# Eight of sixteen first-layer groups in seven products of halves, in place of four, with the steps of a block put in a new order

## The chip, the core and the metric

The kernel runs on one core of a Trainium2 chip. The metric is the device time of one execution, in microseconds (us). The engines are named as the profile names them: PE multiplies matrices, PEld loads its weights, DVE, ACT and POOL are the vector, scalar and general engines, SP only issues DMAs here. Each engine works through its own instructions in order and waits on semaphores for the others.

## The reference

Linear attention with projected keys and values over eight batches, and behind it a feed-forward layer on all tokens. With B = 8 batches, H = 8 heads, S = 1024 tokens, D = 64 and k = 64 projected positions:

```python
k_proj = einsum('ks,bhsd->bhkd', E, k)
v_proj = einsum('ks,bhsd->bhkd', F, v)
attn = softmax(q @ k_proj^T / sqrt(D))          # over the 64 projected positions
x = (attn @ v_proj) as 8192 tokens of H*D = 512
h = x @ w_in                                    # 512 -> 2048
g = h * clip(h + 3, 0, 6) / 6
out = g @ w_out                                 # 2048 -> 512
```

The kernel computes in bf16 with float32 sums; inputs are cast while they are loaded, the output is float32.

## The kernel before

**Blocks.** Each batch b has two blocks, t = 0 and t = 1, of 512 tokens; "block (b,t)" below. PE is kept fed by an order written out by hand: a string of step names such as `L0 A7 L1 A6`, walked once per block. A letter names a piece of work, the number says which part of it. `at(place, ...)` hangs further work (the attention of the next batch) behind a named step, `pop()` after a step takes one postponed instruction from the list `later`, and `behind_steps(n)` postpones an instruction by n steps (the list `soon`, counted down by `step_done`).

**First layer.** A block's h has 2048 columns, done as 16 groups of 128: `first_group` (L0 to L15) is 8 matmuls of 512 columns into a PSUM tile of the pool `ps_mm` (tag "mm", four tiles). `h_out` then makes g from it: ACT writes r = relu(h/6 + 0.5) to a tile of the pool `rpool`, DVE multiplies g = min(r, 1) * h.

**Second layer.** g times w_out for the tokens of a block is done on 2x2 blocks of halves with seven products in place of eight (Strassen's scheme in Winograd's form). `Pair` does this for two of the four rows of output tiles: steps 7, 2, 5, 6, 1, 3 and 4 are the seven products. It needs sums of blocks of g (class `Sums`: a in place on DVE, sb on DVE, sc and sd on POOL) and of w_out (`w_sums`, and b12 and b21 in place). Steps 7, 2 and 5 are copied from PSUM to SBUF by ACT (`copied`, m7, m2, m5), and steps 6, 1, 3 and 4 make the output tiles o_sb of the pool `opool` by a subtraction on DVE or a copy on ACT; each tile is stored by an SP DMA. The second layer of a block runs while the next block's first layer is computed: A and B are the two pairs of the block before, N is the pair A of the present block, of which steps 2 and 5 are done early (N2, N5).

**Quad.** From batch 3 on, four of the sixteen groups (f = 12 to 15) are done together by the same scheme, in seven products of halves: `Quad`, steps Q7, Q2, Q6, Q5, Q1, Q3, Q4, each 8 matmuls of 256 columns. Its sums of x (xc, xa, xb, xd) are made on POOL by `sums`, its sums of w_in lie in `v_sums`, and two blocks of w_in (v12, v21) are replaced by their sums in place in batch 3. Steps 7, 2 and 5 are copied to float32 tiles qm7, qm2, qm5 by ACT; steps 6, 1 and 3 subtract on DVE, and then g is made from the result: Relu on ACT, min and multiply on POOL. Step 4 goes Relu on ACT, multiply on DVE.

**Attention of the next batch.** `second` is the attention whose x is made during this batch: `some_scores` (PE) and exponents (ACT, line 276, from PSUM tiles of the pool `ps_at`, tag "at"), `add_up` (a transposing reduction on DVE, line 308), `sums_turned` (small DVE instructions), `spread_sums` (a reciprocal on DVE, two SP DMAs that write turned_rows to DRAM, eight SP DMAs that spread it over partitions as rec), and in t = 1 `some_values` (PE, then multiplies by rec on DVE, line 300, which give xT). `third` is the attention after that: `projected` is 32 pairs of matmuls on k and v; behind it, one step at a time, the casts of kp (ACT), `turn` (three SP transposing DMAs: kT, and qT twice) and the casts of vp. `load_next` issues the DMAs of the next k, v and q from POOL, behind a small copy, the mark, that waits for qT.

The order of the blocks of batches 3 to 7, and what hangs on it:

```python
    QUADS = ("L0 A7 L1 A6 L2 B7 L3 A1 L4 B2 L5 A3 L6 B5 L7 A4 "
             "L8 Q7 Q2 B6 L9 Q6 N2 Q5 B1 L10 Q1 B3 L11 Q3 N5 B4 Q4").split()
...
            at((0, "L1"), scores(0, 1))
...
            spread((0, "B6"), (0, "B3"))
            if third:
                at((0, "B4"), lambda: third.projected(pause=False))
                if third.b + 1 < B:
                    at((1, "L7"), third.load_next)
```

After the last block the remaining steps of the second layer run in the order `TAIL`. Batches 1 and 2 have the order `ORDER` (the first block `START`), without quads.

Of the kernel before, what the change touches and what calls it, by code (L numbers as in the profile page):

```python
# [15 lines left out]
def kernel(  # L16
# [41 lines left out]
    gpool = ctx.enter_context(tc.tile_pool(name="g", bufs=2))  # L58
    rpool = ctx.enter_context(tc.tile_pool(name="r", bufs=4))
    spool = ctx.enter_context(tc.tile_pool(name="s", bufs=1))  # L60
    opool = ctx.enter_context(tc.tile_pool(name="o", bufs=4))
    ps_mm = ctx.enter_context(tc.tile_pool(name="ps_mm", bufs=4, space=bass.MemoryType.PSUM))
# [75 lines left out]

    NQ, KX = 2, KO // 2
    v11, v12, v21, v22 = [w_in_sb[:, k:k + KX, f * P:(f + NQ) * P] for k in (0, KX) for f in (FO - 2 * NQ, FO - NQ)]  # L140
    v_sums = consts.tile([P, 3, KX, NQ * P], bf16, name="v_sums")

    def sums_of_w_in():
        add(v_sums[:, 0], v11, v21, nc.gpsimd)
        add(v_sums[:, 1], v11, v22, nc.gpsimd)
        sub(v_sums[:, 2], v11, v12, nc.gpsimd)

# [74 lines left out]
    class Attention:  # L222
# [91 lines left out]
        def sums_turned(self):  # L314
            turned, other = [att.tile([P, KO * 32], f32, tag="turned", name="turned", bufs=2) for _ in range(2)]
            inv = att.tile([KP, KO * 32], f32, tag="inv", name="inv", bufs=1)
            nc.vector.transpose(turned, self.parts.rearrange("p j c -> p (j c)"))
            for t in range(NB):
                here, there = slice(t * KP, t * KP + 32), slice(t * KP + 32, (t + 1) * KP)
                nc.vector.tensor_copy(other[here], turned[there])  # L320
                nc.vector.tensor_add(inv[t * 32:(t + 1) * 32], turned[here], other[here])
            self.inv = inv
# [410 lines left out]
    class Quad:  # L733

        def __init__(self, x, t, g, last):
            self.g, self.last = g, last
            self.blocks = [x[:, k:k + KX, t, i * HT:(i + 1) * HT] for i in range(2) for k in (0, KX)]

        def sums(self):
            a11, a12, a21, a22 = self.blocks
            tiles = [spool.tile([P, KX, HT], bf16, tag="x" + name, name="x" + name) for name in "cabd"]
            self.xc, self.xa, self.xb, self.xd = tiles
            add(self.xc, a11, a21, nc.gpsimd)
            sub(self.xa, a22, a21, nc.gpsimd)
            sub(self.xb, a11, self.xa, nc.gpsimd)
            sub(self.xd, a12, self.xb, nc.gpsimd)

        def product(self, n, ps, first=False):  # L750
            a11, a12, a21, a22 = self.blocks
            x, w = {1: (self.xb, v_sums[:, 1]), 2: (a11, v_sums[:, 2]), 3: (self.xd, v22), 4: (a12, v21),
                    5: (self.xc, v12), 6: (self.xa, v11), 7: (a22, v_sums[:, 0])}[n]
            for p in range(NQ):
                for k in range(KX):
                    in_columns(ps[:, p * HT:(p + 1) * HT], w[:, k, p * P:(p + 1) * P], x[:, k],
                               start=(first and p == k == 0), stop=(k == KX - 1),
                               skip_group_check=not first or p > 0)

        def copied(self, name):  # L760
            m = spool.tile([P, TOK], f32, tag="q" + name, name="q" + name)
            nc.scalar.copy(m, self.y)
            return m

        def out(self, h, i, j, engine=None):
            f = FO - 2 * NQ + j * NQ
            g = self.g[:, f:f + NQ, i * HT:(i + 1) * HT]

            def relu():
                r = rpool.tile([P, TOK], f32, tag="r", name="r")  # L770
                nc.scalar.activation(r, h, AF.Relu, bias=0.5, scale=1.0 / 6.0)  # L771
                r3, h3 = [v.rearrange("p (a n) -> p a n", a=NQ) for v in (r, h)]
                if self.last or engine is nc.vector:
                    behind_steps(1)(lambda: nc.vector.scalar_tensor_tensor(g, r3, 1.0, h3, op0=ALU.min, op1=ALU.mult))
                else:
# [5 lines left out]
        def step(self, n):  # L781
            if n in (7, 2):
                self.y = pat()
            elif n == 6:
                self.x = pmm()
            self.product(n, self.y if n in (7, 2, 5) else self.x, n in (7, 2, 6))
            if n == 7:
                self.m7 = self.copied("m7")
            elif n == 2:
                self.m2 = self.copied("m2")  # L790
            elif n == 5:
                self.m5 = self.copied("m5")
            elif n == 6:
                sub(self.m7, self.m7, self.x)
                self.out(self.m7, 1, 0, nc.gpsimd)
            elif n == 1:
                sub(self.m5, self.m5, self.x)
                self.out(self.m5, 1, 1, nc.gpsimd)
            elif n == 3:
                sub(self.m2, self.x, self.m2)  # L800
                self.out(self.m2, 0, 1, nc.gpsimd)
            else:
                self.out(self.x, 0, 0, nc.vector)
# [15 lines left out]
    for what in "A2 A7 V0 B7 A5 V1 A6 R B2 A1 V2 B5 R A3 B6 V3 A4 B1 R".split():  # L819
# [11 lines left out]
        if what in added:  # L831
# [3 lines left out]


    ORDER = ("L0 A7 L1 A6 L2 B7 L3 A1 L4 B2 L5 A3 L6 B5 L7 A4 "
             "L8 L9 B6 L10 N2 L11 B1 L12 N5 L13 B3 L14 L15 B4").split()
    QUADS = ("L0 A7 L1 A6 L2 B7 L3 A1 L4 B2 L5 A3 L6 B5 L7 A4 "
             "L8 Q7 Q2 B6 L9 Q6 N2 Q5 B1 L10 Q1 B3 L11 Q3 N5 B4 Q4").split()  # L840
    START = "L0 B3 L1 L2 B4 L3 L4 L5 L6 L7 L8 L9 L10 N2 L11 L12 L13 N5 L14 L15".split()
    TAIL = "A7 B7 B2 A6 B5 B6 A1 B1 A3 B3 A4 B4".split()

    second = Attention(2)
    for b in range(1, B):
        if b + 1 < B:
            x_next = second.xT = x_tile()
# [31 lines left out]
        elif b == 2:  # L879
# [7 lines left out]
            at((1, "A6"), add_up(3))  # L887
            spread((1, "A1"), (1, "L4"))
            at((1, "L4"), third.projected)
        elif b + 1 < B:  # L890
            if b == 3:
                at((0, "L0"), lambda: add(v12, v12, v22, nc.gpsimd), lambda: sub(v21, v21, v22, nc.gpsimd))
                at((0, "start"), second.load_next)
            at((0, "L1"), scores(0, 1))
            at((0, "B7"), add_up(0))
            at((0, "A1"), scores(2, 3), add_up(1))
            at((0, "A3"), add_up(2))
            at((0, "A4"), add_up(3))
            spread((0, "B6"), (0, "B3"))
            if third:  # L900
                at((0, "B4"), lambda: third.projected(pause=False))
                if third.b + 1 < B:
                    at((1, "L7"), third.load_next)
        if b < 3:
# [6 lines left out]
        elif b + 1 < B:  # L911
            at((1, "L3"), values(0, 1))
            at((1, "L7"), values(2, 3))

# [3 lines left out]

        for t in range(NB):
            g = g_tile()  # L920
            sums = Sums(g)
# [3 lines left out]
            if quads:  # L925
                pairs["Q"] = Quad(xT, t, g, (b, t) == (B - 1, NB - 1))
            if not start:
                behind[0].sums.a(KH - left, KH)
            left = 2 * NQ if quads else 2
            done("start")  # L930
            for what in START if start else QUADS if quads else ORDER:
                n = int(what[1:])
                if what[0] != "L":
                    pairs[what[0]].step(n)
                    step_done()
                    if quads and what[0] in "LQB":
                        pop()
                    done(what)
                    if what == ("N5" if quads else "N5" if start else "B3"):
                        sums.a(0, KH - left)  # L940
                    continue
# [7 lines left out]
                else:  # L949
                    first_group(xT, t, g, n, behind_steps(2) if quads and n >= KH else now)  # L950
                step_done()
                pop()
                if n == KH - 1:
                    sums.c()
                if not start and n == 0:
                    behind[0].sums.b()
                    behind[0].sums.d()
                if quads and n == 0:
                    pairs["Q"].sums()
                done(what)  # L960
            while soon:
                step_done()
# [4 lines left out]
    sums = behind[0].sums  # L967
    sums.a(KH - left, KH)
    sums.b()
    sums.d(nc.vector)  # L970
    for what in TAIL:
        behind["AB".index(what[0])].step(int(what[1:]))

# [29 lines left out]
```

## Time and profile before

| | |
|---|---|
| median of 3 runs | 480.58 us (480.12 to 480.73) |
| the profiled execution | 480.11 us, of which the span is 478.3 us |
| PE busy | 471.1 us, 99%, 6450 matmuls |
| DVE busy | 340.0 us, 71%, 549 instructions |
| POOL busy | 304.4 us, 64%, 206 instructions |
| ACT busy | 275.1 us, 58%, 532 instructions |
| a first-layer group's Relu (ACT, L562), mean | 598 ns |
| its multiply (DVE, L563), mean | 680 ns |
| a quad's min on POOL (L776), mean | 1536 ns |
| a quad's multiply on POOL (L777), mean | 1345 ns |

The profile is one execution. Times in it are counted from the start of the span; the execution's own time is 1.8 us longer than the span. Busy time of the vector engines is the sum of the instructions' durations; where two instructions follow each other without a wait, the record of the second begins a little ahead of the end of the first. The blocks of batches 3 to 7 begin at 191.35, 219.76 (batch 3), 246.81, 275.66 (4), 302.70, 331.55 (5), 358.58, 385.70 (6), 412.73 and 438.37 us (7); the tail begins at 464.45 us. In a listing, L199 is line 199 of the kernel; `mm<-xT,w_in_sb` reads "writes mm, reads xT and w_in_sb".

### The profile page before, as it was taken

The numbers are of one execution on the slowest core, as the hardware profiler recorded it, in microseconds if no ns is written. First come the engines' busy times: TensorE is split into PE (matmuls) and PEld (weight loads), VectorE is DVE, ScalarE is ACT, GpSimd is POOL, SyncE is SP. The second block draws the span as 40 slices with busy tenths as digits, with TensorE's granted clock in tenths as the row PEclk, the third lists the DMA queues.
The fourth block names the chain that finished last, engine by engine and source line by source line (L and its number), as shares of the span: only waits on it lengthen the run. The fifth ranks groups of instructions, "written<-read, shape, count | busy, mean of one in ns | idle before, by whom it ended". The sixth has DMA issues, their size and how long they took to land.

```text
span 478.3 us, 14964 instructions
## 1 busy us (share of the span) xinstructions
PE 471.1 (99%) x6450; PEld 347.1 (73%) x6450; DVE 340.0 (71%) x549; ACT 275.1 (58%) x532; POOL 304.4 (64%) x206
## 2 busy tenths in 40 slices
PE   8899999999999999999999999999999999999997
PEld 4454567667666776787787877778687877878797
DVE  3583387678765958886778867887778897747574
ACT  3666478775447554756466555666457554556451
POOL 8634956144335123877897778887778588788820
PEclk9999999999999999999999999999999999999999
DMA  9999989984976989995999197962931054111012
GB/s 165 197 201 207 239 148 209 161 152 95 226 148 109 208 158 223 201 202 135 222 143 194 48 210 144 209 135 67 210 117 45 24 151 120 45 47 45 30 62 89
DMA packets 84593, 68.65 MB, mean 144 GB/s; under 512 B 38320, under 2 KB 70576, under 8 KB 84528
## 3 DMA queue, kind: packets, MB, share of 16 engines
q0 software_dynamic: 33008, 29.36, 39.4%
q1 hardware_dynamic: 51152, 37.83, 33.0%
q8 instruction: 50, 0.82, 0.7%
q10 hardware_dynamic: 368, 0.52, 0.4%
q14 instruction: 15, 0.12, 0.1%
HBM read 71.83 MB, written 16.97 MB: 186 GB/s over the span
## 4 chain that ended last, share of the span: by engine, by line
PE 82%; DMA 7%; DVE 4%; POOL 2%; ACT 2%; issue 2%; SPq 1%; POOLq 0%; ACTq 0%
PE mm L199 60%; PE at L199 19%; DMA v<-in_v_dram 5%; DMA rec<-turned_rows 1%; PE at L288 1%; DVE g L563 1%; PE at L267 1%; DVE parts L308 1%; ACT aT L276 1%; SPq L335 1%; POOL q L103 1%; POOL k L107 1%; DMA turned_rows<-inv 0%; POOL v L107 0%; DVE xT L300 0%
## 5 line engine op out<-in xcount | busy, mean ns | idle before, releaser
L199 PE MATMUL mm<-xT,w_in_sb 128*64 128x512 bf16 (+1 forms) x1808 | 222.3, 375 | 0.0
L563 DVE SCALAR_TENSOR_TENSOR g<-r,mm 128x512 bf16<-128x512 f32 x216 | 146.1, 680 | 70.8 <-ACT r L562 69.8
L562 ACT ACTIVATE r<-mm 128x512 f32<-128x512 f32 x216 | 128.3, 598 | 114.6 <-PE mm L199 109.0
L199 PEld LDWEIGHTS <-w_in_sb 128*64 128x64 bf16 x2048 | 118.9, 110 | 58.3 <-issue 3.2
L199 PEld LDWEIGHTS <-g 128*64 128x64 bf16 x2048 | 113.5, 110 | 23.9 <-issue 4.1
L133 POOL TENSOR_TENSOR sc<-g 128x2048 bf16<-128x2048 bf16 x14 | 57.0, 4072 | 53.0 <-DVE g L563 53.0
L136 POOL TENSOR_TENSOR sd<-g,sb 128x1024 bf16<-128x1024 bf16 x28 | 59.0, 2126 | 42.4 <-DVE sb L136 40.0
L199 PE MATMUL mm<-w_out_sb,g 128*64 128x256 bf16 (+1 forms) x1088 | 78.1, 286 | 0.1
L199 PE MATMUL at<-w_sums,g 128*64 128x256 bf16 x896 | 59.0, 273 | 0.2 <-DVE g L563 0.2
L776 POOL TENSOR_SCALAR r<-r 128x512 f32<-128x512 f32 x27 | 41.5, 1536 | 15.2 <-ACT r L771 15.2
L692 ACT COPY m<-at 128x256 f32<-128x256 f32 x84 | 31.3, 373 | 32.8 <-PE at L199 28.1
L777 POOL TENSOR_TENSOR g<-r,qm 128x512 bf16<-128x512 f32 x27 | 36.3, 1345 | 2.3
L300 DVE TENSOR_TENSOR xT<-at,rec 128x512 bf16<-128x512 f32 x54 | 34.9, 682 | 2.6 <-DMA rec<-turned_rows 1.9
L199 PE MATMUL mm<-w_out_sb,sd 128*64 128x256 bf16 x480 | 31.4, 273 | 0.1
L136 DVE TENSOR_TENSOR o_sb<-m,mm 128x256 f32<-128x256 f32 x60 | 24.7, 412 | 9.5 <-PE mm L199 7.2
L199 PE MATMUL mm<-w_sums,sb 128*64 128x256 bf16 x480 | 31.3, 273 | 0.0
L276 ACT ACTIVATE aT<-at 128x512 bf16<-128x512 f32 x52 | 29.5, 602 | 2.9 <-PE at L267 2.9
L199 PEld LDWEIGHTS <-sd 128*64 128x64 bf16 x480 | 26.9, 110 | 4.0 <-issue 0.4
L308 DVE TRANSPOSE_TENSOR_REDUCE parts<-aT 128x32 f32<-128x1024 bf16 x24 | 29.6, 1234 | 0.0
L199 PE MATMUL at<-w_out_sb,sc 128*64 128x256 bf16 x448 | 29.6, 273 | 0.0
L199 PEld LDWEIGHTS <-sc 128*64 128x64 bf16 x480 | 26.7, 110 | 3.6 <-issue 0.5
L199 PEld LDWEIGHTS <-sb 128*64 128x64 bf16 x480 | 26.2, 110 | 4.2 <-issue 1.9
(115 smaller groups left out, 496.1 us busy)
## 6 DMA issues: line engine op xcount, KB each, us to landing
out_dram<-o_sb SPq DMA_DIRECT2D x60, 256.0 KB, 4.4
rec<-turned_rows SPq DMA_DIRECT2D x48, 256.0 KB, 5.8
k<-in_k_dram POOLq DMA_DIRECT2D x7, 1024.0 KB, 10.6
v<-in_v_dram POOLq DMA_DIRECT2D x7, 1024.0 KB, 16.3
q<-in_q_dram POOLq DMA_DIRECT2D x7, 1024.0 KB, 21.1
w_out_sb<-in_moe_w_out_dram POOLq DMA_DIRECT2D x4, 512.0 KB, 15.0
w_in_sb<-in_moe_w_in_dram POOLq DMA_DIRECT2D x7, 256.0 KB, 9.7
k<-in_k_dram POOLq DMA_DIRECT2D x4, 256.0 KB, 5.6
```

The lines of the kernel that those rows point to most:

```text
L103: nc.gpsimd.dma_start(out=q0[:, t, hs], in_=kqv_dram["q"][0][:, hs, t * SB:(t + 1) * SB, :])
L133: engine.tensor_tensor(out=out, in0=x, in1=y, op=ALU.add)
L136: engine.tensor_tensor(out=out, in0=x, in1=y, op=ALU.subtract)
L199: nc.tensor.matmul(ps[lo:lo + width], stationary[:, lo:lo + width], moving, **flags)
L276: when(lambda r=r: nc.scalar.activation(aT[:, :, r, :], tiles[r].rearrange("p (a n) -> p a n", a=2), AF.Exp, scale=scale))
L300: when(lambda t=t: nc.vector.tensor_mul(self.xT[:, j, t, :], av[t], rec[:, t]))
L308: nc.vector.tensor_reduce(out=self.parts[:, j], op=ALU.add, axis=mybir.AxisListType.X, apply_transpose=True, in_=self.aT[j].rearrange("p a ...
L562: nc.scalar.activation(r, h_ps, AF.Relu, bias=0.5, scale=1.0 / 6.0)
L563: when(lambda: nc.vector.scalar_tensor_tensor(g[:, fo, :], r, 1.0, h_ps, op0=ALU.min, op1=ALU.mult))
L692: self.copy(m, ps)
L776: nc.gpsimd.tensor_scalar(out=r, in0=r, scalar1=1.0, scalar2=None, op0=ALU.min)
L777: nc.gpsimd.tensor_tensor(out=g, in0=r3, in1=h3, op=ALU.mult)
```

## The change

From batch 3 on a second quad, R, takes groups f = 8 to 11, so that a block has L0 to L7 and two times seven products of halves. Both quads of a block use the same sums of x. The sums of w_in are made for both (in batch 1), the in-place ones for R in batch 2. The last two steps of Q (q3, q4) are done in the next block or the tail. The second factor of g's clip is now done differently: Q's three subtracted blocks have Relu on ACT, and min and multiply in one instruction on DVE; R's steps 6 and 1 have a second Relu on ACT (1 - relu(0.5 - h/6), clipped at 0) and a multiply on POOL, its step 3 is as Q's. The sum a of g is one DVE instruction of 128x2048, in the next block, in place of two of 128x1024. The sums of a block are made at new places (`MADE`), the x tile of the next batch is taken later, and several pools are smaller: r and o_sb three tiles in place of four, `turned` one in place of two, qm2 two in place of one.

The order of the steps, and the places at which the attention's parts hang, are new for these blocks. The core of the diff (left out: the passing of engines to `Quad`, the change of `sums_turned` that writes over `parts`, and places where only names change):

```diff
-    rpool = ctx.enter_context(tc.tile_pool(name="r", bufs=4))
+    rpool = ctx.enter_context(tc.tile_pool(name="r", bufs=3))
...
-    opool = ctx.enter_context(tc.tile_pool(name="o", bufs=4))
+    opool = ctx.enter_context(tc.tile_pool(name="o", bufs=3))
...
-    NQ, KX = 2, KO // 2
+    NQ, KX, NQUADS = 2, KO // 2, 2
+    v_blocks = [[w_in_sb[:, k:k + KX, f * P:(f + NQ) * P] for k in (0, KX) for f in (FO - (2 * i + 2) * NQ, FO - (2 * i + 1) * NQ)]
+                for i in range(NQUADS)]
...
+    def sums_in_place(i):
+        v11, v12, v21, v22 = v_blocks[i]
+        add(v12, v12, v22, nc.gpsimd)
+        sub(v21, v21, v22, nc.gpsimd)
...
-        def copied(self, name):
-            m = spool.tile([P, TOK], f32, tag="q" + name, name="q" + name)
+        def copied(self, name, y):
+            m = spool.tile([P, TOK], f32, tag="q" + name, name="q" + name, bufs=2 if name == "m2" else 1)
...
-                nc.scalar.activation(r, h, AF.Relu, bias=0.5, scale=1.0 / 6.0)
+                nc.scalar.activation(r, h, AF.Relu, bias=0.5, scale=(-1.0 if engine is nc.scalar and not self.last else 1.0) / 6.0)
...
-                if self.last or engine is nc.vector:
-                    behind_steps(1)(lambda: nc.vector.scalar_tensor_tensor(g, r3, 1.0, h3, op0=ALU.min, op1=ALU.mult))
+                if engine is nc.scalar and not self.last:
+                    nc.scalar.activation(r, r, AF.Relu, bias=1.0, scale=-1.0)
+                    nc.gpsimd.tensor_tensor(out=g, in0=r3, in1=h3, op=ALU.mult)
+                elif self.last or engine is nc.vector:
+                    behind_steps(2)(lambda: nc.vector.scalar_tensor_tensor(g, r3, 1.0, h3, op0=ALU.min, op1=ALU.mult))
...
-    QUADS = ("L0 A7 L1 A6 L2 B7 L3 A1 L4 B2 L5 A3 L6 B5 L7 A4 "
-             "L8 Q7 Q2 B6 L9 Q6 N2 Q5 B1 L10 Q1 B3 L11 Q3 N5 B4 Q4").split()
+    QUADS = ("L0 q3 L7 A7 L5 q4 L1 B7 A6 L3 L2 L6 A1 B2 R7 L4 B6 B5 "
+             "A3 R2 R6 B1 R5 N2 A4 Q2 R1 Q7 Q6 B3 Q5 R3 Q1 N5 R4 B4").split()
+    MADE = {'L1': 'x', 'R2': 'c', 'q3': 'a', 'B2': 'd', 'A6': 'b'}
+    LAST = {'q3': 'ab', 'A6': 'd'}
+    ENGINES = ((nc.vector, nc.vector, nc.vector), (nc.scalar, nc.scalar, nc.vector),)
...
-    TAIL = "A7 B7 B2 A6 B5 B6 A1 B1 A3 B3 A4 B4".split()
+    TAIL = ("q3 B2 q4 A7 B7 A6 B6 "
+             "A1 B5 B1 A3 B3 A4 B4").split()
...
-        if b + 1 < B:
+        if b + 1 < B and b < 4:
             x_next = second.xT = x_tile()
...
-            at((0, "L1"), scores(0, 1))
-            at((0, "B7"), add_up(0))
-            at((0, "A1"), scores(2, 3), add_up(1))
-            at((0, "A3"), add_up(2))
+            at((0, "q3"), scores(0, 1))
+            at((0, "L6"), add_up(0))
+            at((0, "L3"), scores(2, 3))
+            at((0, "B5"), add_up(1))
+            at((0, "R7"), add_up(2))
             at((0, "A4"), add_up(3))
-            spread((0, "B6"), (0, "B3"))
+            spread((0, "Q2"), (0, "Q6"))
             if third:
-                at((0, "B4"), lambda: third.projected(pause=False))
+                at((0, "Q2"), lambda: third.projected(pause=False))
                 if third.b + 1 < B:
-                    at((1, "L7"), third.load_next)
+                    at((1, "B1"), third.load_next)
...
             at((1, "L3"), values(0, 1))
-            at((1, "L7"), values(2, 3))
+            at((1, "B5"), values(2, 3))
...
+            if t and 3 < b < B - 1:
+                x_next = second.xT = x_tile()
...
-            left = 2 * NQ if quads else 2
+            left = 8 if quads else 2
...
-                    if what == ("N5" if quads else "N5" if start else "B3"):
+                    sums_made()
+                    if what == ("B5" if quads else "N5" if start else "B3") and left < KH:
                         sums.a(0, KH - left)
...
-                    first_group(xT, t, g, n, behind_steps(2) if quads and n >= KH else now)
+                    first_group(xT, t, g, n, behind_steps(1) if quads and n >= KH else now)
...
-                if not start and n == 0:
+                if not quads and not start and n == 0:
                     behind[0].sums.b()
                     behind[0].sums.d()
-                if quads and n == 0:
-                    pairs["Q"].sums()
...
-            while soon:
+            while soon and not quads:
                 step_done()
```

## The prediction

> **What bounds it now.** I read the page's busy table and slice rows first, then the windows of the blocks that change, then the order of time on PE, SP and POOL. "Block (b,t)" is half t of batch b; the ten blocks of batches 3 to 7 change.
>
> ```profile
> span 478.3 us, 14964 instructions
> PE 471.1 (99%) x6450; PEld 347.1 (73%) x6450; DVE 340.0 (71%) x549; ACT 275.1 (58%) x532; POOL 304.4 (64%) x206
> PEclk9999999999999999999999999999999999999999
> ```
>
> ```profile
> 302.70:331.55 28.85, 28.85 (x428) 22.61 (x426) 24.29 (x36) 18.05 (x37) 22.92 (x15) 1.00 0.66 133
> 331.55:358.58 27.03, 27.03 (x394) 21.19 (x392) 19.36 (x33) 15.25 (x30) 20.49 (x14) 1.00 0.75 162
> 358.58:385.70 27.12, 27.12 (x412) 21.48 (x410) 23.64 (x36) 17.44 (x36) 20.69 (x13) 1.00 0.12 41
> ```
>
> The columns of the windows are length, then busy PE, PEld, DVE, ACT, POOL. These are blocks (5,0), (5,1), (6,0). PE has no hole in any of them and the clock is full throughout, so only fewer matmul columns shorten a block, and any new wait of PE is paid in full. DVE is next: 84% to 87% in t=0, 72% in t=1.
>
> ```profile
> 313.20 1.03 PE L199 MATMUL mm<-xT,w_in_sb 128*64 128x512 bf16 x8
> 314.06 1.04 PE L199 MATMUL mm<-w_out_sb,sd 128*64 128x256 bf16 x16
> 314.93 1.03 PE L199 MATMUL mm<-xT,w_in_sb 128*64 128x512 bf16 x8
> 321.88 0.60 PE L199 MATMUL mm<-xa,w_in_sb 128*64 128x256 bf16 x8
> 322.32 1.04 PE L199 MATMUL at<-w_sums,g 128*64 128x256 bf16 x16
> ```
>
> Start to start, a first-layer group (L) costs 0.866 us, a second-layer product 0.871, and a product of a quad (four groups done in seven products) 0.436.
>
> **PE.** Per block four L (3.464) become seven quad products (3.052): 0.412 saved, over ten blocks 4.1 us. The built order shows the 240 additional matmuls this means, so the change does what it says. By columns alone (1,024 of 8,192) it would be 0.433 per block, 4.3 in all.
>
> The Trainium skill (TensorE: Matmul & The Clock Gate, "Wait — 56ns, not 53.3ns?") gives each warm matmul a fixed cost of about 2.5 ns, which speaks against cutting matmuls in two; an estimate with it is 16 x 215.8 less 28 x 109.2 ns, 0.396 per block, close to the rows' 0.412.
>
> In four t=0 blocks the product of Q1 stood 0.11 longer (0.55, not 0.44) waiting on DVE. Now B3, Q5 and R3 (1.74 us of PE) lie between Q6 and Q1; of the 0.4 I take 0.2 off, as DVE is fuller there.
>
> **DVE, ACT, POOL per block.** DVE: three more subtractions (0.69) and two more multiplies (0.68), and the in-place subtraction of g becomes one of 128x2048 (1.23) in place of two of 128x1024 (0.86 each, 1.73): +2.9 busy. ACT: three more copies (0.59), four more Relu on sums for four on L, and two second Relu (0.63): about +3.0. POOL loses three min (1.54) and one multiply (1.35): -6.0. So (6,0) has 26.5 of 26.7 us on DVE by busy time, which looks full. But those durations overlap: on DVE's timeline from 283.05 a multiply of 0.69 is followed by the next start after 0.61, and that xT product of 0.68 after 0.60; the small o_sb subtraction (0.41) takes some 0.33 by the same share. Counted start to start, (6,0) is 14 multiplies and 6 subtractions at 0.60, 6 small ones at 0.33, 2.3 for a and sb, 4 reductions at 1.16, 2.6 for the turned sums, 0.9 for the reciprocal: 24.4 of 26.7. It fits, with little to spare.
>
> **Walk of the waits.** I laid out one t=0 and one t=1 block by hand in the new order: PE steps at 0.866, 0.871, 0.436 (projection 1.72, scores or values 0.67 with their gaps), 0.21 from a PE end to its reader, Relu and copies 0.5 start to start, DVE as above. Where DVE or ACT free a PSUM tile or make an operand, the slack in us is:
> - A6 on the in-place subtraction: 1 to 2. A1 on sb: 0.7. L6 on q4's multiply: 0.7. B1 on B6's subtraction: 0.7.
> - R4 on R3's subtraction in t=0 of batches 3 to 5, where the reciprocal stands ahead of it on DVE: 0.
> - (3,0): POOL now sums in place (2 x 1.15) and makes four x sums (4.7) ahead of sd. Its last DMA issue ends at 194.9, so sd's second half is ready at 206.1, and A3 needs it at about 206.2: 0.
>
> Price of these: from 0 (all hold) to 0.15 x ten; I take 0.4. The three-deep r and o pools instead of four free in time by the same walk, but for one, next.
>
> **The queue of SP.** This is what the diff hides. `third.projected` now follows Q2, and the reciprocal with its DMAs only Q6. So on SP the transposes of kT and qT stand ahead of turned_rows and the eight rec loads; before they stood behind:
>
> ```profile
> 272.70 0.80 SPq L329 DMA_DIRECT2D turned_rows<-inv  x2
> 274.75 5.15 SPq L335 DMA_DIRECT2D rec<-turned_rows  x8
> 280.00 0.54 SPq L696 DMA_DIRECT2D out_dram<-o_sb  x1
> 280.65 1.30 SPq L250 DMA_TRANSPOSE kT<-kp  x1
> 282.05 8.65 SPq L187 DMA_TRANSPOSE qT<-q  x2
> ```
>
> Block (4,1) begins at 275.66, so rec was issued 0.9 before it, and its first pair was used at 283.66. An earlier batch has the transposes with no rec ahead of them:
>
> ```profile
> 139.21 1.23 SPq L250 DMA_TRANSPOSE kT<-kp  x1
> 140.53 5.70 SPq L187 DMA_TRANSPOSE qT<-q  x2
> 146.33 2.08 SPq L696 DMA_DIRECT2D out_dram<-o_sb  x2
> ```
>
> There the second qT was issued at 142.59 and landed 5.7 later, 9.1 after kT's issue. In the new order kp is ready 4.3 before the block's end (projection 5.7 before it, two casts 1.06, handover 0.25), qT lands at +4.8, and rows, issued at +2.7, can't be read before that: rec starts at about +5.1, six later than now. The first pair of rec landed 5.1 after its start in (4,0): +10.2. The values now come at 7.8 into t=1, DVE reaches their multiply at about 10.1, and B2, which needs its PSUM tile, starts at 11.1. So the cover just suffices. Price: 0 if it holds, 2 per block if qT takes the 8.65 of the first fence; I take 0.2 (nearest the second fence), three blocks (batches 3 to 5): 0.6.
>
> The out store of B.lo queues behind the rec loads too, and with three o_sb tiles A3's subtraction in t=1 waits for its landing: the store at 280.00 landed 7.3 later, 12.6 after rec's start, so at +17.7, where DVE would have been ready at 16.8. R6's subtraction behind it slips to 18.7, and with that:
>
> **The queue of POOL.**
>
> ```profile
> 295.52 0.18 POOL L217 COPY mark<-qT 1x1 bf16<-1x1 bf16 x1
> 295.64 0.99 POOL L121 DMA_DIRECT2D k<-in_k_dram  x1
> 296.62 0.89 POOL L121 DMA_DIRECT2D v<-in_v_dram  x1
> 297.49 0.91 POOL L121 DMA_DIRECT2D q<-in_q_dram  x1
> ```
>
> `load_next` moves from L7 to B1 of t=1. Its mark and three issues hold POOL for 2.9 us, now between the multiply of R6 and that of R1. ACT's copy of Q5 waits for R1's multiply (same buffer), and ACT is in order: copy, Relu of R3 and Q1, the o_sb copy, Relu of R4 and L0, the first exponent. By the walk R1's multiply ends at 26.0, the copy is 2.2 late, and the exponent that frees A7's tile in the next t=0 comes 0.6 after A7 would start. Price: 0 to 1.2 each (below: if A3's wait is shorter; above: if it is 1 longer), taken 0.6, for the two batches that load (3 and 4): 1.2. The loads themselves keep cover: q lands about 22 after k's issue, that is near 17.5 of the next t=0, and is needed at 25.
>
> The Trainium skill (DMA: Bandwidth & Descriptors, "Queues, rings and completion order") says descriptors of a ring are consumed in order and a completion lands only after the earlier writes; the store landing 0.7 after the last rec here agrees, and were the queues independent the SP term would be 0.
>
> First blocks: three more sums on POOL at 1.15 lie in a hole of 13.9 us before batch 1's sc. The tail keeps its products, and q3, B2, q4 only move into it: A6 waits for the subtraction of g, with 3.5 us of PE ahead of it: 0.
>
> **Sum.** 480.11 (this execution; 478.3 of span and 1.8 around) - 4.1 - 0.2 + 0.4 + 0.6 + 1.2 = 478.0. The median of the runs stands 0.47 above this execution: 478.5.
>
> **Rivals.**
> - All covers hold: -4.1 to -4.3 and up to 0.4 from Q1, 475.9 to 476.5. For it: PE had no waits in these blocks before. Against: four slacks of zero or less in the walk. 0.17.
> - Slower: the rec handover is late. Place: SP in t=0 of batches 3 to 5. If the transposes take 2.95 longer (first fence), B2 stands 2.0 in three blocks (6.0), and A3's wait grows alike, so that ACT holds A7 another 1.0 twice: 484 to 486. It decides from qT landing 11 us after kT's issue rather than 9.1. For it: qT was never faster with traffic ahead. Against: with rec behind, the ring is empty. 0.18.
> - DVE becomes the bound: if DVE durations count in full, four t=0 blocks give back 1 to 1.5 each on top: 480 to 483.5. For it: 26.5 of 26.7. Against: start-to-start 0.60. 0.15.
> - The forecast case: 477.3 to 479.8. 0.50.
>
> **Numbers.** About 0.2% (0.96 us) is what a measurement of this kernel can tell from no change. Faster than 479.6: nearly all of forecast and first rival, 0.63. Within: edges of forecast and the DVE case, 0.16. Slower than 481.5: the handover and the rest of DVE, 0.21. The range 475.9 to 483.0 leaves out most of the handover case and little else.
>
> **What would show it.** Right: changed blocks shorter by 0.41 on PE; in the waits, PE at A7 of (4,0) and (5,0) behind the exponent; SP with kT, qT, rows, rec in this order and rec about 5 into t=1; DVE waiting on an out store before A3. Wrong: PE holes over 1 us at B2 in t=1 (handover), or holes spread over all t=0 blocks behind DVE multiplies (DVE bound), or PE solid and 476.2.

## The result, and the profile after

The changed kernel takes 486.37 us (median; 486.11 to 486.58), the kernel before beside it 480.56: a ratio of 1.0122, 95% interval 1.0105 to 1.0140. It is slower by 5.8 us where 2 us less were forecast. The profiled span went from 478.3 to 484.7. The page's busy table:

```profile
span 484.7 us, 15486 instructions
PE 472.8 (98%) x6690; PEld 357.1 (74%) x6690; DVE 368.6 (76%) x578; ACT 299.1 (62%) x580; POOL 266.6 (55%) x175
PEclk9999999999999999999999999999999999999999
```

DVE is 28.6 us busier (2.9 for each of the ten blocks); PE has holes now. The windows of blocks (5,0), (5,1) and (6,0), columns as before:

```profile
305.73:334.07 28.34, 28.34 (x454) 23.43 (x451) 25.10 (x37) 21.64 (x44) 16.54 (x11) 1.00 0.79 151
334.07:362.29 28.22, 27.66 (x421) 22.44 (x418) 24.25 (x39) 16.69 (x35) 16.51 (x9) 1.00 0.57 139
362.29:388.90 26.61, 26.61 (x437) 22.53 (x434) 25.44 (x38) 19.63 (x39) 16.19 (x10) 1.00 0.12 43
```

The t=0 blocks, where DVE looked fullest, are solid and 0.51 shorter. The t=1 block between them is 1.19 longer (28.22, before 27.03), though DVE has less to do in it. Against before, DVE's busy time rose by 0.8 in (5,0) (24.29 to 25.10) and by 4.9 in (5,1) (19.36 to 24.25). All blocks, start of L0 to start of L0, against what 0.41 less and the 0.87 of q3 and q4 (which leave (3,0) and enter the tail) would give:

| block | before | after | above the sum |
|---|---|---|---|
| (3,0) | 28.41 | 29.81 | 2.7 |
| (3,1), (4,1), (5,1) | 27.05, 27.04, 27.03 | 28.23, 28.22, 28.22 | 1.6 each |
| (4,0), (5,0), (6,0) | 28.85, 28.85, 27.12 | 28.33, 28.34, 26.61 | -0.1 each |
| (6,1) | 27.03 | 27.88 | 1.3 |
| (7,0), (7,1) | 25.64, 26.08 | 25.86, 25.86 | 0.6, 0.2 |
| tail | 13.85 | 16.20 | 1.5 |

These come to 10.7 us; less 4.1 of saving and a start 0.2 earlier, that is the 6.4 of the spans. The view of waits names only the long ones (it keeps the short holes inside a product out):

```profile
PE mm L206 <- POOL sd L136: 1.0, 1, 1.0
PE mm L206 <- DVE sb L136: 1.0, 1, 1.0
PE mm L206 <- DVE o_sb L136: 0.9, 2, 0.7
PE mm L206 <- ACT o_sb L738: 0.9, 3, 0.3
PE mm L206 <- DVE g L571: 0.6, 3, 0.2
```

The first two are block (3,0), the third is the tail, the last two the starts of (3,1), (4,1) and (5,1). One such start, (4,1), on PE's timeline: L0, q3, L7, A7, L5.

```profile
277.51 1.03 PE L206 MATMUL mm<-xT,w_in_sb 128*64 128x512 bf16 x8
278.44 0.63 PE L206 MATMUL mm<-xd,w_in_sb 128*64 128x256 bf16 x8
279.36 1.05 PE L206 MATMUL mm<-xT,w_in_sb 128*64 128x512 bf16 x8 [0.29 <-ACT o_sb L738]
280.23 1.16 PE L206 MATMUL at<-w_sums,g 128*64 128x256 bf16 x16
281.57 0.81 PE L206 MATMUL mm<-xT,w_in_sb 128*64 128x512 bf16 x5 [0.19 <-DVE g L571]
```

Start to start q3 takes 0.92 in place of 0.436, and A7 1.34 in place of 0.871: 0.95 lost in these steps. L7 waits for the PSUM tile that ACT's copy of B4 frees. ACT and DVE at the same time:

```profile
278.42 0.63 ACT L783 ACTIVATE r<-qm 128x512 f32<-128x512 f32 x1 [0.39 <-DVE qm L136]
278.96 0.35 ACT L738 COPY o_sb<-mm 128x256 f32<-128x256 f32 x1
```

```profile
276.66 1.13 DVE L789 SCALAR_TENSOR_TENSOR g<-r,qm 128x512 bf16<-128x512 f32 x1 [0.63 <-ACT r L783]
277.71 0.68 DVE L136 TENSOR_TENSOR qm<-qm,mm 128x512 f32<-128x512 f32 x1
278.31 2.60 DVE L789 SCALAR_TENSOR_TENSOR g<-r,qm 128x512 bf16<-128x512 f32 x2
280.84 0.67 DVE L571 SCALAR_TENSOR_TENSOR g<-r,mm 128x512 bf16<-128x512 f32 x1
```

ACT's copy stands behind a Relu that waits for DVE's subtraction, and that stands behind a multiply of 1.13 us. The three multiplies of the quad Q (L789) take 3.73 us, though a multiply of the same size that reads PSUM (L571) takes 0.67 right after them. The reason is on POOL:

```profile
276.09 1.15 POOL L133 TENSOR_TENSOR xc<-xT 128x512 bf16<-128x512 bf16 x1
277.20 1.60 POOL L136 TENSOR_TENSOR xa<-xT 128x512 bf16<-128x512 bf16 x1
278.89 1.48 POOL L136 TENSOR_TENSOR xb<-xT,xa 128x512 bf16<-128x512 bf16 x1
```

The first multiply starts at 276.66 inside xc, which ends at 277.24; the multiply ends 0.55 after that. Then xa, begun at 277.20, takes 1.60 and not 1.15. The two engines take turns. Over the whole trace from batch 3 on, L789 on operands in SBUF takes 0.68 with POOL idle and 1.20 with POOL busy beside it (0.86 to 1.65); L571, which reads PSUM, 0.674 and 0.676. The Trainium skill (SBUF — State Buffer, "Who interferes with whom") states it: a DVE instruction with two inputs in SBUF and a GpSimd instruction that reads SBUF exclude each other for the whole instruction, while one with at most one SBUF input, outside the two-port modes of DVE, does not contend. The rows of L789 and L571 agree with both halves.

### The profile page after: what moved, and what is told of

It is laid out like the page before. It is cut to its first block, busy times and chain, and to the rows that moved or that the text cites. A ratio compares the mean times of both kernels' runs of the same rounds, so it can differ in the third digit from the quotient of the medians.

```text
span 484.7 us, 15486 instructions
## 1 busy us (share of the span) xinstructions
PE 472.8 (98%) x6690; PEld 357.1 (74%) x6690; DVE 368.6 (76%) x578; ACT 299.1 (62%) x580; POOL 266.6 (55%) x175
## 4 chain that ended last, share of the span: by engine, by line
PE 66%; DVE 18%; DMA 5%; POOL 4%; ACT 3%; issue 2%; SPq 1%; DVEq 0%; ACTq 0%; POOLq 0%
PE mm L206 44%; PE at L206 17%; DVE g L789 5%; DVE g L571 4%; DVE qm L136 2%; DVE g L136 1%; DVE sb L136 1%; PE at L295 1%; DMA qT<-q 1%; DMA g<-in_F_dram 1%; DVE parts L315 1%; DVE o_sb L136 1%; PE at L274 1%; DMA rec<-turned_rows 1%; DVE xT L307 1%
## 5 line engine op out<-in xcount | busy, mean ns | idle before, releaser
L206 PE MATMUL mm<-xT,w_in_sb 128*64 128x512 bf16 (+1 forms) x1568 | 183.5, 369 | 1.6 <-ACT o_sb L738 0.9
L206 PEld LDWEIGHTS <-w_in_sb 128*64 128x64 bf16 x2048 | 116.4, 110 | 58.7 <-issue 9.9
L571 DVE SCALAR_TENSOR_TENSOR g<-r,mm 128x512 bf16<-128x512 f32 x176 | 117.6, 680 | 46.8 <-ACT r L570 46.0
L570 ACT ACTIVATE r<-mm 128x512 f32<-128x512 f32 x176 | 104.4, 598 | 70.6 <-PE mm L206 55.4
L774 ACT COPY qm<-at 128x512 f32<-128x512 f32 x60 | 34.9, 582 | 25.0 <-PE at L206 18.2
L783 ACT ACTIVATE r<-qm 128x512 f32<-128x512 f32 x60 | 37.8, 630 | 12.3 <-DVE qm L136 12.2
L789 DVE SCALAR_TENSOR_TENSOR g<-r,qm 128x512 bf16<-128x512 f32 x42 | 42.5, 1027 | 2.1 <-ACT r L783 1.9
L136 DVE TENSOR_TENSOR qm<-qm,mm 128x512 f32<-128x512 f32 x40 | 27.3, 686 | 19.6 <-PE mm L206 15.4
L307 DVE TENSOR_TENSOR xT<-at,rec 128x512 bf16<-128x512 f32 x54 | 35.9, 682 | 3.7 <-PE at L295 1.7
L787 POOL TENSOR_TENSOR g<-r,qm 128x512 bf16<-128x512 f32 x18 | 22.9, 1274 | 28.0 <-ACT r L786 27.9
```

The costliest lines, as they stand in the source:

```text
L136: engine.tensor_tensor(out=out, in0=x, in1=y, op=ALU.subtract)
L206: nc.tensor.matmul(ps[lo:lo + width], stationary[:, lo:lo + width], moving, **flags)
L307: when(lambda t=t: nc.vector.tensor_mul(self.xT[:, j, t, :], av[t], rec[:, t]))
L570: nc.scalar.activation(r, h_ps, AF.Relu, bias=0.5, scale=1.0 / 6.0)
L571: when(lambda: nc.vector.scalar_tensor_tensor(g[:, fo, :], r, 1.0, h_ps, op0=ALU.min, op1=ALU.mult))
L774: nc.scalar.copy(m, y)
```

## Experiments

Theory C is this contention at the turn of a block; rival A is ACT's order there; rival D is DVE's bare count of instructions. Block (3,0) waits for sb by 0 to 1 us from run to run (it hangs on when POOL, which waits for qT, gets to the sums of x: sb takes about 2.1 or about 3.2 there), so the table gives, beside the median, the profiled stretch from L0 of (3,1) to the end of the span, which is free of that.

| kernel | median | from (3,1) on |
|---|---|---|
| before | 480.56 | 258.54 |
| changed | 486.37 | 263.75 |
| sums of x behind sd | 496.9 | 275.16 |
| sums of x twice | 497.61 | 274.67 |
| one quad | 486.26 | 264.33 |
| tail's tiles | 484.65 | 262.94 |
| mark | 483.9 | 261.70 |
| sums of x once | 482.69 | 260.60 |
| projection behind B4 | 482.31 | 260.11 |
| casts alone behind B4 | 484.91 | 262.68 |
| three edits | 481.63 | 259.59 |
| four edits | 477.25 | 258.04 |
| the same, x behind sd in (3,0) | 481.33 | 257.99 |
| four edits without the mark | 479.28 | 259.03 |

**All sums of x behind sd.**

```diff
-    MADE = {'L1': 'x', 'R2': 'c', 'q3': 'a', 'B2': 'd', 'A6': 'b'}
+    MADE = {'R2': 'c', 'q3': 'a', 'B2': 'dx', 'A6': 'b'}
```

> The changed kernel with one edit: the four sums of x on POOL stand behind sd (step B2) and not at L1, so that they no longer run while DVE multiplies the quad Q's results at the turn of a block. Theory C (POOL's sums of x lengthen DVE's multiplies whose operands all lie in SBUF, 0.68 us alone, 0.86 to 1.65 beside them, and the sb of block (3,0), 3.18 us beside them, 1.21 alone): those multiplies fall to 0.68 to 0.70, sb of (3,0) to 1.2, block (3,0) loses 1.5 to 2.5 us, the t=1 blocks of batches 3 to 6 about 1.2 each, the blocks of batch 7 about 0.3 each: 478.5 to 480.5 us. Rival A (ACT is late at the turn because of its casts of kp and vp and its second Relus, and PE waits for ACT's order): the multiplies get shorter but the PE waits at L7 and A7 of t=1 stay; only sd of (3,0) comes earlier, 1 us: 485 to 485.5. Rival D (DVE has simply too many instructions in the first 16 us of a t=1 block): the part of 1.8 us per block that contention adds goes, and half of the waits stay: 482 to 483.5.

Measured 496.9 us (496.15 to 497.15), 10.5 more, outside all three ranges. At the turns into (3,1), (4,1) and (5,1) the multiplies did fall to 0.69 (at the other turns the first still took 0.97 to 2.25, beside a late multiply of R on POOL), sb of (3,0) fell to 1.22, and (3,0) became 28.5. But sc, pushed later, now ran beside `sums_turned`. DVE's timeline in t=0 of batch 4, then the line of the waits:

```profile
269.34 2.60 DVE L328 COPY parts<-turned 32x128 f32<-32x128 f32 x1
271.97 1.25 DVE L329 TENSOR_TENSOR inv<-turned,parts 32x128 f32<-32x128 f32 x1
```

```profile
PE mm L206 <- DVE qm L136: 8.5, 14, 2.0
```

The copy took 0.78 in the changed kernel and the addition 0.28. That is contention moved to a place in the middle of the quads' subtractions. It is not the whole loss: block (7,0), which has no `sums_turned`, became 2.4 longer. There POOL does R6's multiply only behind sc; ACT's copy of Q7, which takes the same buffer, waits for it, DVE's subtraction of Q6 for the copy, and PE for the subtraction:

```profile
446.18 1.27 POOL L787 TENSOR_TENSOR g<-r,qm 128x512 bf16<-128x512 f32 x1
```

```profile
447.49 0.58 ACT L774 COPY qm<-at 128x512 f32<-128x512 f32 x1 [2.96 <-POOL g L787]
```

```profile
448.10 0.69 DVE L136 TENSOR_TENSOR qm<-qm,mm 128x512 f32<-128x512 f32 x1 [2.97 <-ACT qm L774]
```

```profile
448.85 0.63 PE L206 MATMUL mm<-xb,v_sums 128*64 128x256 bf16 x8 [1.88 <-DVE qm L136]
```

So the edit changed two things, the overlap and the order of POOL's queue, and its time decides between no theories.

**The sums of x twice.**

```diff
+            for _ in range(1 if (b, t) == (3, 0) else 2):
-            add(self.xc, a11, a21, nc.gpsimd)
+                add(self.xc, a11, a21, nc.gpsimd)
...
```

> The changed kernel with the four sums of x done twice (same results) in every block of batches 3 to 7 but (3,0). In t=1 POOL has 6.5 us of waiting before sd, so the second pass of 4.7 us delays nothing of POOL's own there. Theory C: the second pass lies beside more of DVE's instructions with operands in SBUF alone (the in-place subtraction of 1.21, the multiplies of Q3 and the start of sb), each longer by 30 to 100 per cent: 1 to 2.5 us more in each t=1 block and up to 1 in t=0: 491 to 502 us. Rivals A and D: DVE and ACT have the same work, so no more than 1 us, 486 to 487.5.

Measured 497.61 us (496.53 to 498.83), +11.2, inside C's range and far from A's and D's. DVE has not one instruction more; the second pass falls on the in-place subtraction and the multiply of Q3, as in (4,1) here, and in six other blocks on sb, 1.88 there and 1.21 in the changed kernel:

```profile
285.79 1.50 DVE L136 TENSOR_TENSOR g<-g 128x2048 bf16<-128x2048 bf16 x1
288.41 1.68 DVE L790 SCALAR_TENSOR_TENSOR g<-r,qm 128x512 bf16<-128x512 f32 x1
```

**One quad in the new order.** `NQUADS` 1, R's steps replaced by L8 to L11.

```diff
-    ... B2 R7 L4 B6 B5 A3 R2 R6 B1 R5 N2 A4 Q2 R1 Q7 Q6 B3 Q5 R3 Q1 N5 R4 B4
+    ... B2 L8 L4 B6 B5 A3 L9 B1 N2 A4 Q2 L10 Q7 Q6 B3 Q5 L11 Q1 N5 B4
```

> The changed kernel without the second quad: groups 8 to 11 are first-layer groups again, at the places where R's steps stood (L8 at R7, L9 at R6, L10 at R1, L11 at R3); the new order, Q's multiplies on DVE, the smaller pools and all places of the sums and of the attention stay. Theory C: PE's saving of 0.41 in ten blocks is gone (+4.1) and the waits at the turn of t=1 stay nearly whole, since Q's three multiplies still lie beside the sums of x: 488 to 491 us. Rival A (second Relus and copies of R burden ACT): without R's three copies, two second Relus the waits fall by half or more: 483 to 486. Rival D: DVE has 0.6 us less per block, waits fall by a third: 486 to 488.

Measured 486.26 us (486.16 to 487.04): C's number missed by 2, D's hit, A's missed by 0.3. The wait at A7 stayed (for a multiply of Q, six times: the four t=1 blocks of batches 3 to 6 and both of batch 7; in (4,1) A7 took 1.46, 0.59 too much), that at L7 went, B2's too. So the new order, with Q's multiplies on DVE and the smaller pools, costs the 5.8 us by itself; the second quad took 4.1 from PE and gave as much back in waits.

**The tail's low tiles from another pool.**

```diff
-                self.lo = opool.tile([P, d_model], f32, tag="o_sb", name="o_sb")
+                self.lo = (rpool.tile([P, d_model], f32, tag="r", name="r") if self.final else
+                           opool.tile([P, d_model], f32, tag="o_sb", name="o_sb"))
```

> The changed kernel with one edit in the last block's pairs alone: the tile of the low rows (lo) is taken from the pool r, not from the pool o with its three tiles. Theory: in the tail DVE's last subtraction waited 1.50 us for the landing of an out store whose tile it takes, and PE's last product 0.69 for that; with the other tile that wait goes, 0.7 to 0.9 us: 485.4 to 485.7. Rival (the last product waits on DVE's order anyway): 486.2 to 486.4, no change.

Measured 484.65 us (483.6 to 485.41), 1.7 less where 0.7 to 0.9 were expected. From (3,1) on it is 0.8, and that is the wait (PE's last two products took 2.83, now 1.94). The profiled run gains another 0.4 ahead of (3,1); the rest of the median's 1.7 no profile shows. The row of the changed kernel that goes, and its reason, that with three o_sb tiles the one it takes is still being stored:

```profile
480.04 0.42 DVE L136 TENSOR_TENSOR o_sb<-mm,m 128x256 f32<-128x256 f32 x1 [1.50 <-DMA out_dram<-o_sb]
```

**A mark ahead of the sums of x.**

```diff
         def sums(self, *others):
+            if (b, t) != (3, 0):
+                mark = att.tile([1, 1], bf16, tag="mark", name="mark")
+                nc.gpsimd.tensor_copy(mark, pairs["q"].g[:1, FO - 1, TOK - 1:])
```

> The changed kernel with one instruction more per block (all of batches 3 to 7 but (3,0)): ahead of the sums of x POOL copies one element of what Q's step 1 wrote to g in the block before, so that the sums begin only when DVE is through with the three multiplies of the turn (about 2.7 us later than now, and still 4 us ahead of sd). No other queue's order moves. Theory C: the three multiplies fall from 1.13, 1.04 and 1.64 to about 0.69, DVE's backlog at the start of t=1 is 1.8 us shorter, less 0.4 to 0.8 that now falls on the in-place subtraction and a multiply of Q3; of the 1.6 us that each t=1 block lost 1.0 to 1.3 go, of the 0.6 of each block of batch 7 about 0.4: 480 to 482 us. Rival A (ACT's order at the turn): multiplies shorter, waits as before: 485.5 to 486.5. Rival D (too many instructions on DVE): about half of it: 483 to 484.5.

Measured 483.9 us (481.66 to 486.13): 2.5 less, 2.1 of it from (3,1) on. DVE and POOL at the start of (4,1):

```profile
274.81 0.69 DVE L792 SCALAR_TENSOR_TENSOR g<-r,qm 128x512 bf16<-128x512 f32 x1 [0.63 <-ACT r L786]
275.42 0.69 DVE L136 TENSOR_TENSOR qm<-qm,mm 128x512 f32<-128x512 f32 x1
276.02 1.47 DVE L792 SCALAR_TENSOR_TENSOR g<-r,qm 128x512 bf16<-128x512 f32 x2
...
289.82 0.69 DVE L307 TENSOR_TENSOR xT<-at,rec 128x512 bf16<-128x512 f32 x1 [1.09 <-DMA rec<-turned_rows]
```

```profile
277.56 0.18 POOL L753 COPY mark<-g 1x1 bf16<-1x1 bf16 x1 [3.29 <-DVE g L792]
277.70 1.14 POOL L133 TENSOR_TENSOR xc<-xT 128x512 bf16<-128x512 bf16 x1
```

The multiplies are at 0.69, q3 takes 0.57 in place of 0.92 and A7 its 0.87: C's mechanism, and the two blocks of batch 7 fall to 25.2. But the time lies in D's range, 2 above C's. In (4,1), with the turn free, DVE comes early enough to wait 1.09 for rec, and that block still falls to 27.52. (5,1) and (6,1) stay at 28.32 and 28.18: there the later sums meet the multiply of Q3. DVE and POOL in (5,1):

```profile
338.26 1.69 DVE L792 SCALAR_TENSOR_TENSOR g<-r,qm 128x512 bf16<-128x512 f32 x1
```

```profile
338.25 1.16 POOL L136 TENSOR_TENSOR xd<-xT,xb 128x512 bf16<-128x512 bf16 x1
```

In (4,1) the two start as close together, at 282.18 and 282.17, but there the multiply takes 0.69 and xd 1.72. So a part of what is left above C's range is the same contention a little later, and not D's count. Why the eleven runs lie 4.5 us apart stays open: which of the two goes first, worth 0.7 to 1.0 us a block here, could do it, and so could rec's landing; no run tests either.

**The sums of x made once** (a bound, not a version).

```diff
+            if (b, t) == (3, 0):
-            add(self.xc, a11, a21, nc.gpsimd)
+                add(self.xc, a11, a21, nc.gpsimd)
...
```

> The changed kernel with POOL's four sums of x made in block (3,0) alone; the other nine blocks use those of (3,0) again, so their quads' products are not those of their own x. Everything else is as it was. It bounds from above what the contention costs outside (3,0). Theory C: no multiply of Q is over 0.70, the t=1 blocks lose 0 to 0.5 instead of 1.6: 479.5 to 481.5 us. Rival D: 483 to 484. Rival A: 485.5 to 486.5.

Blocks from (3,1) on multiply with the sums of (3,0). Measured 482.69 us (481.17 to 485.09), between C's range and D's. From (3,1) on that is 3.2 less: so much the sums of x cost there, and the mark gets 2.1 of it. The t=1 blocks still stand 0.6 to 1.5 above the sum, so the rest of the 10.7 is something else.

**The projection at the end of t=0 again.**

```diff
-                at((0, "Q2"), lambda: third.projected(pause=False))
+                at((0, "B4"), lambda: third.projected(pause=False))
```

> The changed kernel with the projection of keys and values at the end of t=0 again (behind B4, not Q2), and so the casts of kp and vp on ACT in the first steps of t=1, and on SP turned_rows and rec ahead of the transposes. Theory C (and the forecast's steps on SP and POOL, which would be worth 0 by it): the turn's multiplies stay at 1.0 to 1.6 us and A7's wait stays; what L7 gains is lost to the casts a few us later: 485.5 to 487.5. Rival A: without the 2.2 us of casts ahead of the Relus of Q6 and Q1 the waits at L7 and A7 of three t=1 blocks go: 483 to 484.8. The forecast's steps (rec later because of the transposes, 0.6; load_next between R6 and R1, 1.2): the first comes back: about 485.8.

Measured 482.31 us (481.45 to 482.94): 4.1 less (3.6 from (3,1) on), more than A gave and against C, whose range is missed by 3. Yet the multiplies at the turn still take 0.98 and 2.43 for two. Blocks (3,1), (4,1), (5,1) no longer wait at L7, A7 or B2. Two things had moved, so the next run parts them.

**The casts alone moved, the projection's matmuls left.**

```diff
+                at((0, "Q2"), lambda: third.project(pat))
+                at((0, "B4"), lambda: third.casts())    # keys_out; later: turn, values_out twice
```

> The changed kernel with the projection's matmuls where they are (behind Q2), but the casts of kp and vp and the transposes behind them moved to the end of t=0 (behind B4): ACT's and SP's order as in the run with the whole projection there, PE's order as in the changed kernel. It tells apart why that run was 4 us faster: theory A (ACT was late at the turn because of the casts): the gain stays whole, 482 to 483.5 us. Theory P (the projection's 1.72 us of PE at the turn are work that needs neither DVE nor ACT, and DVE catches up behind it): the waits at L7 and A7 stay in three t=1 blocks, 484.8 to 486.5 us.

Measured 484.91 us (484.36 to 485.79): P's range, at its lower end. L7's wait is gone (the casts had held ACT). The one behind A7 stays: L5 waits for the multiply that frees its PSUM tile:

```profile
277.32 1.03 PE L206 MATMUL mm<-xT,w_in_sb 128*64 128x512 bf16 x8
278.19 1.04 PE L206 MATMUL at<-w_sums,g 128*64 128x256 bf16 x16
279.58 0.62 PE L206 MATMUL mm<-xT,w_in_sb 128*64 128x512 bf16 x4 [0.36 <-DVE g L575]
```

So of the 3.6 us that moving the whole projection gains from (3,1) on, 1.1 are the order of ACT (and SP), and 2.6 are the projection's 1.72 us of PE in each of three turns, as work for which neither DVE nor ACT is needed. (This run also holds the projection's PSUM tile longer, but none of PE's long waits in it is for such a tile.)

**Versions put together.** First the mark, the tail's tiles, and in (3,0) alone the sums of x behind sd:

> Three edits together: the mark ahead of the sums of x (as in the run with it alone), in block (3,0) the sums of x behind sd, and the tail's lo tiles from the pool r. By theory C they add: 4 to 6 us of the mark, 1.3 of (3,0) (which gained that in the run with all x sums behind sd: 29.8 to 28.5), 1.2 of the tail (1.2 in the spans): 477.5 to 480 us, at or below the kernel before. If DVE's count alone decides (D): 481 to 482.5.

481.63 us (480.25 to 482.77): the range of 477.5 to 480 is missed, the number given for D hit. Block (3,0) waited again behind `sums_turned` beside sc, and (5,1) for an xT multiply. Then with the projection behind B4, and for (3,0) two ways; the first is

```diff
-                at((0, "start"), second.load_next)
+                at((0, "B7"), second.load_next)
```

> Four edits together: the mark ahead of the sums of x, the projection behind B4, the tail's lo tiles from the pool r, and in block (3,0) load_next behind B7 instead of at the start, so that POOL no longer stands waiting for qT with the sums in place, the sums of x and sd behind it. From the waits left in the runs with one edit each: three t=1 blocks 1.1 better each, (6,1) 0.7, the two of batch 7 0.6 each, the tail 1.2, block (3,0) 1.2 to 2.3: 477 to 479 us, below the kernel before by 0.3 to 0.7 per cent. If contention or DVE's count comes back in another place: 480 or more.

477.25 us (476.62 to 478.02), ratio to before 0.9935, interval 0.9922 to 0.9949: as expected, and below both kernels. What is left of PE's long waits from batch 3 on, and the window of (4,1), which takes 26.93 (28.22 in the changed kernel) with DVE busy for 20.96 (there 24.23):

```profile
PE mm L206 <- DVE g L571: 0.4, 1, 0.4
PE mm L206 <- DVE o_sb L136: 0.2, 1, 0.2
```

```profile
273.41:300.34 26.93, 26.93 (x418) 22.52 (x416) 20.96 (x35) 17.10 (x35) 19.23 (x14) 1.00 0.84 177
```

The second way keeps load_next and puts the sums of x behind sd there:

> As the run with four edits, but in block (3,0) load_next stays at the start and the sums of x stand behind sd there (as in the earlier combination, where that block still waited 0.5, 0.2, 0.4 and, at the turn, 0.5 us). The projection at the turn covers the last two: 478 to 480 us, 0.5 to 1 above the run with load_next moved.

481.33 us (479.97 to 481.9), above its 478 to 480: in (3,0) PE waited 2.1 at R3 for the subtraction of R1, which stood on DVE behind `sums_turned` (its copy took 2.63 beside sc), for the third time. ACT's copy of Q7 again waited for R6's multiply behind sc, by 2.6; an estimate from these rows is that without the contention 1.7 of PE's wait would have come one step later, at Q1. Last, the best version without its mark:

> The best version (four edits) without the mark: the projection behind B4, the tail's lo tiles from the pool r, load_next of block (3,0) behind B7. It tells what the contention still costs once the projection covers the turn of three t=1 blocks. By the waits in the run with the projection moved alone: (6,1) 0.7 and the two blocks of batch 7 0.5 each are uncovered, block (3,0) unchanged by the mark: 478.3 to 479.3 us. If the covered turns lose by contention too: 480 or more. If the mark gave nothing beside the other edits: 477 to 477.6.

479.28 us (478.87 to 479.62). By the medians the mark is worth 2.0 even when the projection covers three turns, but only 1.0 of it lies from (3,1) on, where the mark stands; without it (6,1) and batch 7 wait as in the changed kernel.

## Why the prediction was wrong, step by step

**PE's saving: right.** (4,0), (5,0) and (6,0) became 0.51 to 0.52 shorter: 0.41 and the 0.11 of Q1.

**DVE: the failing step.** The busy sum's +2.9 per block was hit, but by luck. A block has one more multiply on DVE, not two (in all 238, before 229). What made up for it is lengthening beside POOL: 28 of the quads' multiplies took 1.20 on average where 0.68 would do, 14.6 us, of which sb and other rows, lengthened less than before, give a part back. And the busy times of page and windows, unlike what the section on the profile before says, count time in which two records overlap once (the durations of DVE's rows add up to 397.8 us, the page has 368.6): the discount of "Counted start to start" took off an overlap that was not in them. For (6,0) it gave 24.4; the window shows 25.44. It took 0.60 for each of Q's new multiplies. The row they needed was one with all operands in SBUF and POOL at work beside it. The profile of before had such rows; on DVE and POOL in (4,0):

```profile
250.20 2.25 DVE L136 TENSOR_TENSOR sb<-g 128x2048 bf16<-128x2048 bf16 x1
```

```profile
250.09 1.27 POOL L777 TENSOR_TENSOR g<-r,qm 128x512 bf16<-128x512 f32 x1
```

The same sb takes 1.21 where POOL is idle. I had used 1.23 and 0.86 for g's subtractions without asking why such rows differ. The walk's 0.4 for all slacks was to hold what could go wrong here; the sums of x cost 3.2 outside (3,0).

**The place.** I looked for DVE's limit in t=0, by the largest busy sum. It was in the first steps of t=1, because the projection no longer stood there. Of that move I priced what it did to SP and nothing of what it did to PE and ACT: 2.6 and 1.1 us by the runs.

**(3,0): right place, slack of 0, but two waits.** sd came 2.5 later than walked. q's issue ended at 196.65, not 194.9, as POOL waited longer for qT, and the sums of x ran beside sb:

```profile
199.07 3.18 DVE L136 TENSOR_TENSOR sb<-g 128x2048 bf16<-128x2048 bf16 x1
```

```profile
198.90 1.15 POOL L133 TENSOR_TENSOR xc<-xT 128x512 bf16<-128x512 bf16 x1
201.24 2.02 POOL L136 TENSOR_TENSOR xb<-xT,xa 128x512 bf16<-128x512 bf16 x1
```

I gave this no term of its own. The block came out 2.7 above the sum; the waits for sb and sd, 1.0 each, are 2.0 of it. With load_next behind B7 the block has no wait for sb or sd at all.

**The tail: 0 forecast, 1.5 measured**, 0.9 of it the missing fourth o_sb tile. I had asked that of t=1 and not of the tail.

**SP and POOL: the order right, the price 0.** rec's issue began 5.2 after the start of (4,1), walked as 5.1:

```profile
273.13 1.24 SPq L257 DMA_TRANSPOSE kT<-kp  x1
274.47 5.73 SPq L194 DMA_TRANSPOSE qT<-q  x2
280.30 1.00 SPq L337 DMA_DIRECT2D turned_rows<-inv  x2
282.75 5.16 SPq L343 DMA_DIRECT2D rec<-turned_rows  x8
```

DVE was later still, so rec was not awaited; with the mark it was, by 1.09. load_next stood between R6's and R1's multiplies, and no wait at A7 of (4,0) or (5,0) followed: the 0.6 and 1.2 of the forecast were not there. A wait of the kind that the second was to come from, a copy on ACT held by R's multiply on POOL, reached PE by itself only in the first experiment, where sc stood ahead of that multiply (1.88 in (7,0)). The rival that came nearest by its mechanism is that of DVE as the bound, though in the wrong half of the batch and for another reason. By its number, 484 to 486, the rec handover came nearest, and that is luck: it was not what made it slower.

**Not settled.** The parts measured one by one (the sums of x beside DVE at most 3.2, the projection's place 3.6, the tail 0.9, (3,0) up to 2.7) overlap, since one cover hides more than one delay; they are not to be added up.

## What to carry to other kernels

Before work goes from POOL to DVE, sort DVE's rows by where their operands lie and by what POOL does beside them; a duration from a PSUM operand (0.67) held here for SBUF operands only while POOL was idle (0.68, else 0.86 to 1.65). Count an engine's fill where PE has least other work (here the first steps of a block), not per block. When a step is moved, price also what it covered where it stood, and what now stands behind it in its engine's queue.

## What the hardware showed that was not expected

A DVE multiply on SBUF operands and a POOL sum took turns, each waiting for the other's end (0.68 became 1.65, 1.15 became 2.13 where the sums were made twice). A small DVE copy of 32x128 float32, with one input in SBUF, went from 0.22 to 2.60 beside POOL's sc; the second half of the rule above does not cover it unless it ran in one of those two-port modes, and no run here shows in which mode it ran. None of it shows as a wait: it is inside the busy time of both engines.
